# Longer DMA runs for q and k in a fused attention and gated-MLP kernel: four tokens to a run, order restored on chip

## Chip, cores and metric

The kernel runs on one core of a Trainium2 chip. The metric is the device time of one execution in microseconds (us); lower is better. Before the change it is 248.72 us, the median of three runs (248.6 to 251.48). A run counts as slow when it is over 1.5% above the fastest of the same kernel.

## The reference, cut to what matters

```python
def _attn_ref(q, k, v):                     # each (8, 8, 576, 64) float32: B, H, S, D
    # S is cut into chunks of 64 tokens; attention stays inside a chunk
    scores = scale * np.matmul(q_c, k_c.transpose(0, 1, 2, 4, 3))
    attn = softmax(scores)                   # (cut)
    return np.matmul(attn, v_c).reshape(B, H, S, D)

def reference(**kwargs):
    attn_out = _attn_ref(q, k, v)
    x = attn_out.transpose(0, 2, 1, 3).reshape(B, S, H * D)
    h = np.maximum(x @ w_in, 0.0); u, v = split(h)
    v_n = layer_norm(v)
    v_s = einsum('ts,bsd->btd', w_spatial, v_n) + b_spatial
    return (u * v_s) @ w_out                 # (8, 576, 512) float32
```

The inputs lie in HBM head by head: for one head, 64 floats (256 bytes) of a token are followed by those of the next token. The kernel works on tiles of 128 tokens with all 8 heads, 36 tiles in all. Four of them straddle two batches (576 is four and a half tiles) and are loaded in two pieces of 64 tokens.

## The kernel before

Loads, with tokens on the partitions, so that each contiguous run in HBM is 256 bytes:

```python
    att_in = pool("att_in", 4);  att_bf = pool("att_bf", 3);  osb_pool = pool("osb_pool", 4)
    # ...
    def load(t):
        for name, src in (("q", q), ("k", k), ("v", v)):
            f = att_in.tile([128, H, D], FP32, name=f"{name}f")
            for r0, n, b, s in pieces(t):
                nc.sync.dma_start(out=f[r0:r0 + n],
                                  in_=src[b, :, s:s + n, :].rearrange("h s d -> s h d"))
    # cast(t): GpSimd casts q, k, v to bf16
    # TR(t):   8 TensorE transposes of q and k into one PSUM tile; VectorE copies it out
    # QK(t):   16 score matmuls of 64x64; ScalarE takes the exponential
    # AV(t):   attention x v and the division; XT(t): 4 transposes, ScalarE copies to xT
    # HV, U:   first MLP matmuls;  LN, LN_apply: layer norm (apply is on GpSimd)
    # SP(b):   spatial matmuls of batch b;  FIN(t): last matmul, then
        o_sb = osb_pool.tile([128, d_model], FP32, name="o_sb")
        nc.scalar.copy(o_sb, po)
        nc.sync.dma_start(out=out_flat[t * 128:(t + 1) * 128, :], in_=o_sb)
```

The main loop fixes the order of TensorE and GpSimd by hand, with a model clock:

```python
        for s in range(NT + 3):
            if PRE <= s + PRE - 1 < NT and s > 0:
                load(s + PRE - 1)             # three tiles ahead
            while ln_todo:
                LN_apply(ln_todo.pop(0))      # GpSimd: waits for the statistics
            if 0 < s and s + 1 < NT:
                cast(s + 1)                   # GpSimd: one tile ahead
            # TR(s), XT, QK(s), AV(s-1), with HV / U / SP / FIN filled in between
```

The softmax here doesn't subtract the row's maximum and nothing guards it: scores larger than these inputs give would overflow.

## Time and profile before

| | before |
|---|---|
| median | 248.72 us |
| span of the profiled run | 247.3 us |
| TensorE busy | 204.3 us (83%) |
| DMA | 40.36 MB, mean 163 GB/s |
| GpSimd casts waiting for q and k | 18.7 us |

First the page's rows by time: 40 equal slices of the span, for each the busy share in tenths of TensorE (PE), of its granted clock (PEclk), of the 16 DMA engines on average, and the rate in GB/s; then the line of the hardware DMA queue (packets, megabytes, share of the time of 16 engines) and the issues (KB each, median us from issue to landing).

```profile
PE   0237756599199499999998899999979999999993
PEclk9999996559869979999999999999999999999999
DMA  8999999899249998069977799989738640050225
GB/s 155 211 189 208 175 219 209 181 219 211 50 101 213 188 220 179 34 185 214 193 184 176 166 204 245 255 180 191 196 107 190 111 170 3 0 209 5 85 85 212
...
q1 hardware_dynamic: 117696, 37.76, 69.7%
...
qf<-in_q_dram SPq DMA_DIRECT2D x32, 256.0 KB, 5.0
kf<-in_k_dram SPq DMA_DIRECT2D x32, 256.0 KB, 5.0
vf<-in_v_dram SPq DMA_DIRECT2D x32, 256.0 KB, 5.3
```

In the first quarter the DMA engines are full at some 200 GB/s while TensorE has gaps; from the middle on TensorE is nearly full. The table of stretches has the same in numbers (busy us with the count of instructions, of TensorE's matmuls and weight loads, VectorE, ScalarE and GpSimd in this order; then granted clock, DMA share, GB/s):

```profile
0.00:20.00 20.00, 5.54 (x77) 3.64 (x78) 2.58 (x11) 3.06 (x4) 7.92 (x18) 1.00 1.01 185
20.00:40.00 20.00, 13.00 (x164) 7.94 (x161) 8.76 (x19) 4.93 (x9) 10.21 (x17) 0.97 1.20 200
40.00:60.00 20.00, 16.39 (x177) 9.95 (x176) 7.61 (x17) 5.43 (x10) 4.30 (x7) 0.61 1.05 205
...
140.00:160.00 20.00, 19.91 (x257) 12.10 (x255) 11.94 (x31) 12.15 (x23) 8.02 (x14) 1.00 1.08 236
```

The table of waits (engine, line, tile, what it waited for: us in all, times, longest; POOL is GpSimd, ACT ScalarE, DVE VectorE, SPq the queue in which SyncE issues DMAs) shows how little the casts wait for q and k, how long GpSimd waits for layer-norm statistics, and that the copies into the output buffers wait for TensorE, not for stores:

```profile
POOL vn L258 <- DVE nmu L238: 64.3, 6, 16.2
...
POOL kb L141 <- DMA kf<-in_k_dram: 9.5, 8, 3.5
POOL qb L141 <- DMA qf<-in_q_dram: 9.2, 5, 4.5
...
ACT o_sb L300 <- PE big L297: 22.4, 34, 5.2
```

### The profile page before, as it was taken

How to read it: one execution, taken by the hardware profiler on the slowest of the kernel's cores; microseconds unless marked ns; L12 is line 12 of the kernel's file. 1: busy time of each engine (PE TensorE's matmuls, PEld its weight loads, DVE VectorE, ACT ScalarE, POOL GpSimd, SP SyncE). 2: the span in 40 equal slices, each digit the busy share in tenths (PEclk: the TensorE clock that was granted, in tenths of full speed). 3: DMA queues.
4: the chain of work that ended last, by engine and by line, in shares of the span. 5: the costliest groups of instructions: out<-in, count | busy, mean ns of one | idle time of the engine just before them, and what ended most of it. 6: DMA issues, size and time to landing. Idle time of an engine off the chain costs nothing.

```text
span 247.3 us, 5971 instructions
## 1 busy us (share of the span) xinstructions
PE 204.3 (83%) x2402; PEld 124.8 (50%) x2402; DVE 120.2 (49%) x305; ACT 105.6 (43%) x197; POOL 100.7 (41%) x166
## 2 busy tenths in 40 slices
PE   0237756599199499999998899999979999999993
PEld 0124435345155366566555555755556557446651
DVE  0124254434443667368635663874466548425530
ACT  2011230036227523762564276437643662864133
POOL 4515463300890794009801943395056400524000
PEclk9999996559869979999999999999999999999999
DMA  8999999899249998069977799989738640050225
GB/s 155 211 189 208 175 219 209 181 219 211 50 101 213 188 220 179 34 185 214 193 184 176 166 204 245 255 180 191 196 107 190 111 170 3 0 209 5 85 85 212
DMA packets 119994, 40.36 MB, mean 163 GB/s; under 512 B 113248, under 2 KB 115360, under 8 KB 119968
## 3 DMA queue, kind: packets, MB, share of 16 engines
q1 hardware_dynamic: 117696, 37.76, 69.7%
q0 software_dynamic: 2272, 2.24, 5.9%
q8 instruction: 18, 0.29, 0.5%
q14 instruction: 8, 0.07, 0.1%
HBM read 32.79 MB, written 9.44 MB: 171 GB/s over the span
## 4 chain that ended last, share of the span: by engine, by line
PE 49%; POOL 7%; issue 5%; DMA 4%; DVE 3%; SPq 2%; ACT 1%; POOLq 0%; ACTq 0%
PE big L281 13%; PE big L297 10%; PE big L265 9%; PE big L209 8%; DMA vf<-in_v_dram 4%; PE tr L151 4%; PE o L178 2%; PE tr L191 2%; PE sc L164 2%; SPq L132 2%; POOL vn L258 2%; POOL kb L141 2%; POOL qb L141 2%; DVE bst L215 1%; POOL vaug L141 1%
## 5 line engine op out<-in xcount | busy, mean ns | idle before, releaser
L258 POOL TENSOR_SCALAR vn<-v_relu,rstd,nmu 128x512 bf16<-128x512 f32 x32 | 25.1, 796 | 81.4 <-DVE nmu L238 64.3
L212 ACT ACTIVATE v_relu<-big 128x512 f32<-128x512 f32 x36 | 21.5, 597 | 58.9 <-PE big L209 49.7
L154 DVE COPY qkT<-tr 128x1024 bf16<-128x1024 bf16 x36 | 24.6, 684 | 44.2 <-PE tr L151 44.2
L281 PE MATMUL big<-wsf,vn 128*128 128x288 bf16 x256 | 40.5, 286 | 2.8 <-DVE gat L288 2.6
L215 DVE BATCH_NORM_STATS2 bst<-v_relu 128x6 f32<-128x512 f32 x36 | 24.9, 693 | 34.7 <-ACT v_relu L212 34.6
L209 PE MATMUL big<-w_in_sb,xT 128*128 128x512 bf16 x144 | 40.6, 414 | 0.0
L265 PE MATMUL big<-xT,w_in_sb 128*128 128x512 bf16 x144 | 35.6, 390 | 0.0
L297 PE MATMUL big<-w_out_sb,gat 128*128 128x512 bf16 (+1 forms) x160 | 34.5, 381 | 0.0
L288 DVE TENSOR_TENSOR gat<-big,uT 128x288 bf16<-128x288 f32 (+8 forms) x96 | 30.0, 351 | 8.2 <-PE big L281 7.2
L194 ACT COPY xT<-tr 128x512 bf16<-128x512 bf16 x36 | 21.0, 584 | 23.2 <-PE tr L191 23.1
L151 PE MATMUL tr<-identb,qb 128*128 128x128 bf16 x144 | 15.6, 238 | 18.3 <-POOL qb L141 17.2
L300 ACT COPY o_sb<-big 128x512 f32<-128x512 f32 x36 | 21.1, 586 | 22.4 <-PE big L297 22.4
L168 ACT ACTIVATE eT<-sc 128x512 bf16<-128x512 f32 x36 | 22.0, 611 | 17.5 <-PE sc L164 17.5
L281 PEld LDWEIGHTS <-vn 128*128 128x128 bf16 x256 | 23.7, 97 | 10.6 <-DVE gat L288 2.5
L141 POOL CAST qb<-qf 128x512 bf16<-128x512 f32 x36 | 22.0, 611 | 16.9 <-DMA qf<-in_q_dram 9.2
L141 POOL CAST vaug<-vf 128x512 bf16<-128x512 f32 x36 | 22.1, 615 | 13.8 <-DMA vf<-in_v_dram 13.8
L141 POOL CAST kb<-kf 128x512 bf16<-128x512 f32 x36 | 22.0, 612 | 13.5 <-DMA kf<-in_k_dram 9.5
L267 ACT ACTIVATE uT<-big 128x512 bf16<-128x512 f32 x36 | 21.3, 597 | 12.3 <-PE big L265 11.6
L184 DVE TENSOR_TENSOR x<-o,rz 128x512 bf16<-128x512 f32 x36 | 24.9, 691 | 0.9
L151 PEld LDWEIGHTS <-qb 128*128 128x128 bf16 x144 | 11.1, 105 | 25.2 <-POOL qb L141 19.2
L209 PEld LDWEIGHTS <-xT 128*128 128x128 bf16 x144 | 14.0, 104 | 14.3 <-issue 2.8
L265 PEld LDWEIGHTS <-w_in_sb 128*128 128x128 bf16 x144 | 13.5, 100 | 14.7 <-issue 1.6
(40 smaller groups left out, 195.0 us busy)
## 6 DMA issues: line engine op xcount, KB each, us to landing
out_dram<-o_sb SPq DMA_DIRECT2D x36, 256.0 KB, 2.1
qf<-in_q_dram SPq DMA_DIRECT2D x32, 256.0 KB, 5.0
kf<-in_k_dram SPq DMA_DIRECT2D x32, 256.0 KB, 5.0
vf<-in_v_dram SPq DMA_DIRECT2D x32, 256.0 KB, 5.3
qf<-in_q_dram SPq DMA_DIRECT2D x8, 128.0 KB, 4.6
kf<-in_k_dram SPq DMA_DIRECT2D x8, 128.0 KB, 4.1
vf<-in_v_dram SPq DMA_DIRECT2D x8, 128.0 KB, 4.2
ws_nat<-in_moe_w_spatial_dram POOLq DMA_DIRECT2D x1, 576.0 KB, 6.7
```

The lines of the kernel that those rows point to most:

```text
L141: nc.gpsimd.tensor_copy(dst, f32[name])
L151: nc.tensor.transpose(ps[:, c:c + 128], st[t][name][:, 2 * m:2 * m + 2, :].rearrange("p h d -> p (h d)"), identb)
L154: nc.vector.tensor_copy(qkT, ps)
L168: nc.scalar.activation(eT, sc[:, :, 0:256], AF.Exp, scale=att_scale)
L184: nc.vector.tensor_tensor(x, o[:, :, 0:64], rz.to_broadcast([128, H, D]), op=ALU.mult)
L209: nc.tensor.matmul(hv, xT[g][:, cb, r * 128:(r + 1) * 128], w_in_sb[:, cb, F:], start=(cb == 0), stop=(cb == 3))
L215: nc.vector.bn_stats(bst, vr)
L258: nc.gpsimd.tensor_scalar(y, vr, rstd[:, j:j + 1], nmu[:, j:j + 1], op0=ALU.mult, op1=ALU.add)
L265: nc.tensor.matmul(hu, w_in_sb[:, cb, fb * 128:(fb + 1) * 128], xT[g][:, cb, :], start=(cb == 0), stop=(cb == 3))
L281: nc.tensor.matmul(vs[:, 0:HS], lhsT, rhs, start=(i == 0), stop=(i == 4))
L288: nc.vector.tensor_tensor(gat[b][:, db, half * HS + done:half * HS + done + n], vs[:, done:done + n], uT[g][:, db, r:r + n], op=ALU.mult)
L297: nc.tensor.matmul(po[r0:r0 + n, :], gat[b][:, jb, s:s + n], w_out_sb[:, jb, :], start=(jb == 0), stop=(jb == 3))
```

## The change

The intent: q and k are loaded in runs of 1 KB, four consecutive tokens of one head, and a partition then holds four tokens of two heads. The order is put right again where k is copied out of PSUM, and by a permutation matrix (in place of the identity) in the transposes of the attention output. GpSimd casts two tiles ahead and before it normalises; the normalising is cut into single tiles; several pools are deeper; copies are shared out differently between VectorE and ScalarE; finished tiles have priority in the order.

The core of the diff (pools and the scheduling helpers cut):

```diff
-    att_bf = pool("att_bf", 3)
+    att_bf = pool("att_bf", 4)
-    relu_pool = pool("relu_pool", 8)
-    vn_pool = pool("vn_pool", 12)
+    relu_pool = pool("relu_pool", 12)
+    vn_pool = pool("vn_pool", 20)
+    permb = consts.tile([128, 128], BF16, name="permb")      # identity, columns permuted (cut)
     def load(t):
-        for name, src in (("q", q), ("k", k), ("v", v)):
-            f = att_in.tile([128, H, D], FP32, name=f"{name}f")
+        for name, src in (("q", q), ("k", k)):
+            f = att_in.tile([128, 2, 4 * D], FP32, name=f"{name}f")
             for r0, n, b, s in pieces(t):
-                nc.sync.dma_start(out=f[r0:r0 + n], in_=src[b, :, s:s + n, :].rearrange("h s d -> s h d"))
+                for e in (0, 1):
+                    nc.sync.dma_start(
+                        out=f[r0:r0 + n, e, :],
+                        in_=src[b, 4 * e:4 * e + 4, s:s + n, :].rearrange("h (p r) d -> h p (r d)", r=4))
+        # v is loaded as before
     def TR(t):
-        nc.vector.tensor_copy(qkT, ps)
+        nc.vector.tensor_copy(qT.rearrange("p r c -> p (r c)"), ps[:, 0:512])
+        kT = att_sb.tile([128, 128, 4], BF16, name="kT")
+        nc.scalar.copy(kT, ps[:, 512:1024].rearrange("p (r c) -> p c r", r=4))
     def QK(t):
-                                 qkT[p0:p0 + 64, 512 + col:512 + col + 64],
-                                 qkT[p0:p0 + 64, col:col + 64], start=True, stop=True)
+                                 kT[p0:p0 + 64, col:col + 16, :].rearrange("p l r -> p (l r)"),
+                                 qT[p0:p0 + 64, :, col:col + 16], start=True, stop=True)
     def XT(t):
-                                x[:, 2 * m:2 * m + 2, :].rearrange("p h d -> p (h d)"), identb)
+                                x[:, 2 * m:2 * m + 2, :].rearrange("p h d -> p (h d)"), permb)
     # main loop
-            while ln_todo:
-                LN_apply(ln_todo.pop(0))
-            if 0 < s and s + 1 < NT:
-                cast(s + 1)
+            if 0 < s and s + 2 < NT:
+                cast(s + 2)
+            for i in range(min(3, len(ln_todo))):
+                LN_apply(*ln_todo.pop(0))
```

More of the change, by code (lines that the diff above doesn't have):

```diff
@@ L47 @@
     persist = pool("persist", 1)
+    xT_pool = pool("xT_pool", 4)
+    uT_pool = pool("uT_pool", 6)
     att_in = pool("att_in", 4)
-    att_bf = pool("att_bf", 3)
+    att_bf = pool("att_bf", 4)
     att_sb = pool("att_sb", 3)
-    relu_pool = pool("relu_pool", 8)
-    vn_pool = pool("vn_pool", 12)
-    tail_pool = pool("tail_pool", 2)
+    relu_pool = pool("relu_pool", 12)
+    vn_pool = pool("vn_pool", 20)
+    tail_pool = pool("tail_pool", 3)
     stat_pool = pool("stat_pool", 3)
     bst_pool = pool("bst_pool", 4)
-    gat_pool = pool("gat_pool", 2)
+    gat_pool = pool("gat_pool", 3)
     osb_pool = pool("osb_pool", 4)
@@ L67 @@
     make_identity(nc, identb)
+    permb = consts.tile([128, 128], BF16, name="permb")
+    for c in (0, 1):
+        nc.vector.tensor_copy(permb[:, c * 64:c * 64 + 64].rearrange("p (l r) -> p l r", r=4),
+                              identb[:, c * 64:c * 64 + 64].rearrange("p (r l) -> p l r", r=4))
     eps_sb = consts.tile([128, 1], FP32, name="eps_sb")
@@ L74 @@
         nc.vector.memset(vaug[i][:, :, 64:65], 1.0)
-    xT = [persist.tile([128, 4, 512], BF16, name=f"xT{g}") for g in range(NG)]
-    uT = [persist.tile([128, 4, 512], BF16, name=f"uT{g}") for g in range(NG)]
+    xT, uT = {}, {}
     w_in_sb = persist.tile([128, 4, d_ff], BF16, name="w_in_sb")
@@ L109, in ws_transpose @@
             s0, n, dst = (512 if p == 0 else 0), 64, ws_tail[p]
-        ps = ps_tr.tile([128, 1024], BF16, name="tr")
+        ps = ps_big.tile([128, 1024], BF16, name="big")
         for tb in range(5):
@@ L114, in ws_transpose @@
                                 ws_nat[:m, tb, s0:s0 + n], identb[:m, :m])
-        nc.vector.tensor_copy(dst[:n, :], ps[:n, 0:S])
+        if (i + p) % 2:
+            nc.vector.tensor_copy(dst[:n, :], ps[:n, 0:S])
+        else:
+            nc.scalar.copy(dst[:n, :], ps[:n, 0:S])
     st = {}
@@ L128, in load @@
         f32 = {}
-        for name, src in (("q", q), ("k", k), ("v", v)):
-            f = att_in.tile([128, H, D], FP32, name=f"{name}f")
+        for name, src in (("q", q), ("k", k)):
+            f = att_in.tile([128, 2, 4 * D], FP32, name=f"{name}f")
             for r0, n, b, s in pieces(t):
-                nc.sync.dma_start(out=f[r0:r0 + n], in_=src[b, :, s:s + n, :].rearrange("h s d -> s h d"))
+                for e in (0, 1):
+                    nc.sync.dma_start(
+                        out=f[r0:r0 + n, e, :],
+                        in_=src[b, 4 * e:4 * e + 4, s:s + n, :].rearrange("h (p r) d -> h p (r d)", r=4))
             f32[name] = f
+        f = att_in.tile([128, H, D], FP32, name="vf")
+        for r0, n, b, s in pieces(t):
+            nc.sync.dma_start(out=f[r0:r0 + n], in_=v[b, :, s:s + n, :].rearrange("h s d -> s h d"))
+        f32["v"] = f
         st[t] = {"f32": f32}
@@ L137, in cast @@
         f32 = st[t].pop("f32")
-        qb = att_bf.tile([128, H, D], BF16, name="qb")
-        kb = att_bf.tile([128, H, D], BF16, name="kb")
+        qb = att_bf.tile([128, 4, 2, D], BF16, name="qb")
+        kb = att_bf.tile([128, 4, 2, D], BF16, name="kb")
         for dst, name in ((qb, "q"), (kb, "k"), (vaug[t % NVB][:, :, 0:64], "v")):
-            nc.gpsimd.tensor_copy(dst, f32[name])
+            x = f32[name]
+            nc.gpsimd.tensor_copy(dst, x if name == "v" else x.rearrange("p e (r d) -> p r e d", r=4))
             for f in after_each:
@@ L144, in cast, with cols @@
         st[t] = {"q": qb, "k": kb}
+    def cols(t, c, m):
+        return c * 64 + m * 16 if len(pieces(t)) == 2 else m * 32 + c * 16
     def TR(t):
@@ L148, in TR @@
         for i, name in enumerate(("q", "k")):
-            for m in range(4):
-                c = i * 512 + m * 128
+            for r in range(4):
+                c = i * 512 + r * 128
                 nc.tensor.transpose(ps[:, c:c + 128],
-                                    st[t][name][:, 2 * m:2 * m + 2, :].rearrange("p h d -> p (h d)"), identb)
-        qkT = att_sb.tile([128, 1024], BF16, name="qkT")
-        nc.vector.tensor_copy(qkT, ps)
-        st[t]["qkT"] = qkT
+                                    st[t][name][:, r].rearrange("p e d -> p (e d)"), identb)
+        qT = att_sb.tile([128, 4, 128], BF16, name="qT")
+        nc.vector.tensor_copy(qT.rearrange("p r c -> p (r c)"), ps[:, 0:512])
+        kT = att_sb.tile([128, 128, 4], BF16, name="kT")
+        nc.scalar.copy(kT, ps[:, 512:1024].rearrange("p (r c) -> p c r", r=4))
+        st[t]["qkT"] = (qT, kT)
     def QK(t):
-        qkT = st[t].pop("qkT")
+        qT, kT = st[t].pop("qkT")
         sc = ps_sc.tile([128, 2, 512], FP32, name="sc")
@@ L162, in QK @@
                 p0, c0 = e * 64, c * 64
-                col = m * 128 + c0
+                col = cols(t, c, m)
                 nc.tensor.matmul(sc[c0:c0 + 64, e, m * 64:m * 64 + 64],
-                                 qkT[p0:p0 + 64, 512 + col:512 + col + 64],
-                                 qkT[p0:p0 + 64, col:col + 64], start=True, stop=True)
+                                 kT[p0:p0 + 64, col:col + 16, :].rearrange("p l r -> p (l r)"),
+                                 qT[p0:p0 + 64, :, col:col + 16], start=True, stop=True)
         eT = att_sb.tile([128, 2, 256], BF16, name="eT")
@@ L178, in AV @@
                 nc.tensor.matmul(o[c0:c0 + 64, h, 0:65],
-                                 eT[c0:c0 + 64, h % 2, (h // 2) * 64:(h // 2) * 64 + 64],
+                                 eT[c0:c0 + 64, h // 4, (h % 4) * 64:(h % 4) * 64 + 64],
                                  va[c0:c0 + 64, h, :], start=True, stop=True)
@@ L191, in XT @@
             nc.tensor.transpose(ps[:, m * 128:(m + 1) * 128],
-                                x[:, 2 * m:2 * m + 2, :].rearrange("p h d -> p (h d)"), identb)
+                                x[:, 2 * m:2 * m + 2, :].rearrange("p h d -> p (h d)"), permb)
         g, r = divmod(t, 4)
-        nc.scalar.copy(xT[g][:, :, r * 128:(r + 1) * 128],
+        if r == 0:
+            xT[g] = xT_pool.tile([128, 4, 512], BF16, name="xT")
+        nc.vector.tensor_copy(xT[g][:, :, r * 128:(r + 1) * 128],
                        ps[:, 0:512].rearrange("p (m s) -> p m s", m=4))
@@ L240, in LN, with LN_apply @@
         ln_st[grp] = (k0, ts, rstd, nmu)
-    def LN_apply(grp):
-        k0, ts, rstd, nmu = ln_st.pop(grp)
-        for j, t in enumerate(ts):
-            vr = relu.pop(t)
-            if t - k0 == 4:
-                te = tail_pool.tile([128, F], BF16, name="tail_e")
-                to = tail_pool.tile([128, F], BF16, name="tail_o")
-                nc.gpsimd.memset(te[64:65, :], 1.0)
-                nc.gpsimd.memset(to[64:65, :], 1.0)
-                nc.gpsimd.tensor_scalar(te[0:64], vr[0:64], rstd[0:64, j:j + 1], nmu[0:64, j:j + 1],
-                                        op0=ALU.mult, op1=ALU.add)
-                nc.vector.tensor_scalar(to[0:64], vr[64:128], rstd[64:128, j:j + 1], nmu[64:128, j:j + 1],
-                                        op0=ALU.mult, op1=ALU.add)
-                tail[grp], tail[grp + 1] = te, to
-            else:
-                y = vn_pool.tile([128, F], BF16, name="vn")
-                nc.gpsimd.tensor_scalar(y, vr, rstd[:, j:j + 1], nmu[:, j:j + 1],
-                                        op0=ALU.mult, op1=ALU.add)
-                vn[t] = y
+    def LN_apply(grp, j):
+        k0, ts, rstd, nmu = ln_st[grp]
+        t = ts[j]
+        vr = relu.pop(t)
+        sc, bi = rstd[:, j:j + 1], nmu[:, j:j + 1]
+        if t - k0 == 4:
+            te = tail_pool.tile([128, F], BF16, name="tail_e")
+            to = tail_pool.tile([128, F], BF16, name="tail_o")
+            nc.gpsimd.memset(te[64:65, :], 1.0)
+            nc.gpsimd.memset(to[64:65, :], 1.0)
+            nc.gpsimd.tensor_scalar(te[0:64], vr[0:64], sc[0:64], bi[0:64], op0=ALU.mult, op1=ALU.add)
+            nc.vector.tensor_scalar(to[0:64], vr[64:128], sc[64:128], bi[64:128],
+                                    op0=ALU.mult, op1=ALU.add)
+            tail[grp], tail[grp + 1] = te, to
+        else:
+            y = vn_pool.tile([128, F], BF16, name="vn")
+            nc.gpsimd.tensor_scalar(y, vr, sc, bi, op0=ALU.mult, op1=ALU.add)
+            vn[t] = y
     def U(g, fb):
@@ L266, in U @@
                              start=(cb == 0), stop=(cb == 3))
+        if fb == 0:
+            uT[g] = uT_pool.tile([128, 4, 512], BF16, name="uT")
         nc.scalar.activation(uT[g][:, fb, :], hu, AF.Relu)
@@ L309, with push, can @@
     seq = [0]
-    def push(ready, cost, emit, after=None):
-        fifo.append([ready, seq[0], cost, emit, after])
+    def push(ready, cost, emit, after=None, pri=1, guard=None):
+        fifo.append([ready, (pri, seq[0]), cost, emit, after, guard])
         seq[0] += 1
+    def can(x):
+        return x[5] is None or x[5]()
     def run(item):
@@ L324, in fill @@
         while got < quota:
-            ok = [x for x in fifo if x[0] <= clock[0]]
+            ok = [x for x in fifo if x[0] <= clock[0] and can(x)]
             if not ok:
@@ L340, in after_hv @@
             LN(grp)
-            ln_todo.append(grp)
+            ln_todo.extend((grp, j) for j in range(n))
             ln_done.add(grp)
@@ L355, in try_sp @@
             sp_pushed.add(b)
-            ready = clock[0] + 6.0
+            ready = clock[0] + 12.0
             for half in (0, 1):
@@ L359, in try_sp, with gat_free @@
                     push(ready, 0.62, lambda b=b, half=half, db=db: SP(b, half, db),
-                         lambda b=b, half=half, db=db: after_sp(b, half, db))
-    fin_pushed = set()
+                         lambda b=b, half=half, db=db: after_sp(b, half, db),
+                         guard=lambda b=b: gat_free(b))
+    fin_pushed, fin_done = set(), set()
+    def gat_free(b):
+        c = b - 3
+        return c < 0 or all(t in fin_done for t in batch_tiles(c))
     def after_sp(b, half, db):
@@ L374, in after_sp @@
                 fin_pushed.add(t)
-                push(clock[0] + 1.2, 0.87, lambda t=t: FIN(t))
+                push(clock[0] + 1.2, 0.87, lambda t=t: FIN(t), lambda t=t: fin_done.add(t), pri=0)
     def after_u(g, fb):
@@ L389 @@
     PRE = 4
-    ARR = [6.7, 11.0, 18.0, 21.5, 25.0, 32.0, 35.5]
+    ARR = [6.0, 10.0, 15.0, 19.0, 23.0, 28.0, 32.0]
     def arrival(t):
-        return ARR[t] if t < len(ARR) else ARR[-1] + 3.5 * (t - len(ARR) + 1)
+        return ARR[t] if t < len(ARR) else ARR[-1] + 2.9 * (t - len(ARR) + 1)
     def after_cast0(name):
@@ L407 @@
         cast(1)
+        cast(2)
+        load_ws()
         for p in (0, 1):
             for i in range(5):
-                push(31.0, 0.4, lambda p=p, i=i: ws_transpose(p, i))
+                push(29.0, 0.4, lambda p=p, i=i: ws_transpose(p, i))
         xt_next = 0
@@ L414 @@
                 load(s + PRE - 1)
-            while ln_todo:
-                LN_apply(ln_todo.pop(0))
-            if 0 < s and s + 1 < NT:
-                cast(s + 1)
-                if s + 1 == 3:
-                    load_ws()
-                if s + 1 == 5:
+            if 0 < s and s + 2 < NT:
+                cast(s + 2)
+                if s + 2 == 4:
                     load_w_out()
+            for i in range(min(3, len(ln_todo))):
+                LN_apply(*ln_todo.pop(0))
             if s < NT:
@@ L450 @@
         while fifo:
-            ok = [x for x in fifo if x[0] <= clock[0]]
-            run(min(ok, key=lambda x: x[1]) if ok else min(fifo, key=lambda x: (x[0], x[1])))
+            can_run = [x for x in fifo if can(x)]
+            ok = [x for x in can_run if x[0] <= clock[0]]
+            run(min(ok, key=lambda x: x[1]) if ok else min(can_run, key=lambda x: (x[0], x[1])))
             while ln_todo:
-                LN_apply(ln_todo.pop(0))
+                LN_apply(*ln_todo.pop(0))
 _INS = ['q', 'k', 'v', 'moe_w_in', 'moe_w_spatial', 'moe_b_spatial', 'moe_w_out']
```

## The prediction

> **What bounds the kernel now.** Two stages. In the table of stretches, the DMA share is 1.01, 1.20 and 1.05 in the first three 20 us, at only 185 to 205 GB/s: 110,592 of the 119,994 packets are the 256-byte runs of q, k and v, 18 ns each at the median (mean 21) in the list of packets. A 768 KB tile takes 3.9 us, TensorE is busy 35 of 60 us, and its clock falls to 0.61. From 100 us on TensorE is busy 18 to 20 of every 20 us: it is the bound. The chain of waits agrees: TensorE 49%, DMA 4%. The last v tile is cast at 196 us; the TensorE order then holds 44 us of work, until 243 us.
>
> **What the change means to do.** 512 KB of each tile go in 1 KB runs: 18,432 packets replace 73,728. A line through the measured 18 ns (256 B) and 83 ns (2 KB stores) gives an estimate of 46 ns for 1 KB; on 16 engines that is 1.5 us for q and k, 2.8 us a tile with v. Were that all, I would expect about 225 us. Copies swap between VectorE and ScalarE, neither the bound; TensorE keeps its 2,402 matmuls.
>
> **Why I expect the opposite.** The new source pattern is (4 heads, 32 rows, 1 KB), its target 128 partitions. The Trainium skill, "DMA: Bandwidth & Descriptors", section "Why a DMA increments its semaphore by 16 and not by 1", says the DMA is spread over the largest k up to 16 that divides the slowest dimension of both sides, on the lowest-numbered k engines. Before, 128 and 128 give 16; the trace agrees: 117,696 hardware-queue packets are 115,200 of data and 2,496 = 16 x 156 completions. Now 4 and 128 give k = 4. No run shows it yet. So q and k go through engines 0 to 3 alone.
>
> Costs on those engines, a tile: 128 packets of 1 KB at 45 ns = 5.8 us; 64 v packets at 19 ns = 1.2 us; together 7.0 us (3.9 before). 36 tiles: 253 us. About 22 output tiles stored meanwhile (8 packets of 84 ns) add up to 15 us, the weights (132 packets of 98 ns) about 8 us. The last load lands near 276 us. It is all on the critical path: TensorE's 5.2 us of work a tile is shorter. After the last tile the TensorE order still holds 44 us (counted from it, same as before), plus cast, store and drain about 5 us.
>
> **Prediction: 324 us; 8 in 10 between 298 and 348. Faster by over 2%: 0.06; within 2%: 0.01; slower: 0.93.**
>
> **What would show it.** The hardware queue holds 61,760 packets (160 q and k issues with 4 completions each), not 63,680 (16 each). Mean rate falls to about 125 GB/s, the queue's share of 16 engines to about 38% although the loads bound the kernel.  The q and k casts on GpSimd wait for DMA, over 100 us in all (18.7 before); TensorE falls to near 65% busy.  Last q cast near 275 us (194 before).
>
> **What would make it wrong.** If the queue spreads by partitions after all (k = 16), TensorE bounds all but the start and the time is 215 to 235 us. If 1 KB packets take 40 or 52 ns, the time moves by -23 or +32 us. If stores and weights overlap with loads, 15 us less. If GpSimd, normalising only behind casts two tiles ahead, delays TensorE, some us more.

## The result, and the profile after

The changed kernel is correct and takes 350.19 us (median of four runs, 348.62 to 354.06), against 248.66 us of the kernel before on the same chip. The ratio is 1.4025 (95% interval 1.3891 to 1.4159). Ratios here are the mean time of one kernel's fast runs over that of the other's in the same rounds, so not quite the ratio of the quoted medians. The direction and the slower loads were predicted; the time is 2 us above the predicted range, because one step of the sum, what follows the last load, was wrong (see below).

The profiled run of the changed kernel (354.06 us) fell 1.6% above the fastest. Differences of that size are not read from it.

```profile
PE   0114356592593678777765039999730059999995
PEclk9999998787577559989897558999985559999999
DMA  3945456333343433434534445444334442101324
GB/s 77 170 107 129 99 125 135 105 107 103 105 122 100 112 106 108 127 108 150 157 106 115 119 154 181 132 127 150 101 107 124 118 154 84 37 3 61 121 88 151
...
q1 hardware_dynamic: 61760, 37.76, 36.7%
...
DMA 51%; PE 21%; SPq 18%; POOL 5%; issue 2%; ACT 0%; POOLq 0%; ACTq 0%
```

The last line is the chain of waits by engine. The hardware queue holds 61,760 packets, exactly the number that 4 completions for each of the 160 q and k loads make; 16 would make 63,680. The mean share of the DMA engines has fallen to mostly 3 to 5 tenths, and yet DMA is half of the chain that ended last. A mean over 16 engines that shows 0.4 can be four engines that are full and twelve that have little to do. The trace does not name the engine of a packet, but its list of packets tells how many 1 KB packets were under way at once: four for half of the time in which there were any, and more than five for 3% of it. (In the two-engine run below it is two for 77% of that time and never more than four; in the sixteen-engine run it is up to 24.)

The stretches and the waits that answer to those shown of before:

```profile
40.00:60.00 20.00, 10.87 (x111) 6.01 (x112) 5.33 (x13) 4.75 (x9) 4.79 (x8) 0.91 0.53 114
...
140.00:160.00 20.00, 15.43 (x178) 8.92 (x180) 9.80 (x26) 9.51 (x18) 4.92 (x8) 0.91 0.42 114
...
260.00:280.00 20.00, 0.00 (x0) 0.00 (x0) 0.00 (x0) 0.00 (x0) 4.98 (x9) 0.53 0.41 111
```

```profile
POOL kb L160 <- DMA kf<-in_k_dram: 84.2, 33, 6.7
...
POOL qb L160 <- DMA qf<-in_q_dram: 71.6, 30, 6.0
...
ACT o_sb L329 <- DMA out_dram<-o_sb: 52.0, 3, 28.5
...
PE big L310 <- ACT o_sb L329: 46.0, 2, 27.4
```

The casts now wait 155.8 us for q and k (18.7 before): that was predicted. What was not: from 260 to 280 us no compute engine but GpSimd does anything, although tiles keep arriving. The last two lines say why. TensorE waits for a PSUM buffer that ScalarE has not emptied, and ScalarE waits for one of the four output buffers, whose store has not landed. The timeline at that place shows what held the store (start, us, engine, line, operation; in brackets the idle time before and its releaser). The first line is the copy that fills the last of the four buffers:

```profile
254.63 0.58 ACT L329 COPY o_sb<-big 128x512 f32<-128x512 f32 x1 [0.28 <-PE big L326]
...
263.61 4.47 SPq L143 DMA_DIRECT2D qf<-in_q_dram  x2
...
270.58 4.87 SPq L143 DMA_DIRECT2D qf<-in_q_dram  x2
...
277.19 0.77 SPq L149 DMA_DIRECT2D vf<-in_v_dram  x1
...
278.05 8.45 SPq L330 DMA_DIRECT2D out_dram<-o_sb  x5
...
285.56 0.58 ACT L329 COPY o_sb<-big 128x512 f32<-128x512 f32 x1 [28.46 <-DMA out_dram<-o_sb]
...
286.19 1.12 PE L310 MATMUL big<-wsf,vn 128*128 128x288 bf16 x4 [27.41 <-ACT o_sb L329]
```

SyncE issues in its order, and in this order the loads of the last tiles come before these stores: the four buffers were filled between 247.1 and 255.2 us, and the first of their stores was issued at 278.05 us. The pair of q loads takes 4.5 to 4.9 us to issue from 256 to 275 us (about 1.2 us in the corrected kernel of the first experiment), which I read as the queue of the full engines pushing back; no run tests that reading. (The waits of TensorE for output copies are 46.0 us in two stalls: this one and an earlier one of 18.6 us.)

When does a tile arrive? The starts of the v casts, in us, taken from the trace's timeline (first, every fifth after it, last), with the end of the span:

```
                    tile 0     5    10    15    20    25    30    35 | span
before                 6.8  35.2  70.5  89.6 119.1 143.5 168.2 195.9 | 247.3
changed               11.5  59.6  96.5 132.9 168.3 207.3 248.4 284.9 | 352.3
```

From tile 6 to tile 20 the changed kernel gets a tile every 7.0 to 7.9 us, close to the 7.0 us of the prediction.

And the packets of the hardware queue, from the list of packets in the trace (ns):

```
                 size    count   10th pct  median  mean
before           256 B  110592      18       18    21.0
changed          256 B   36864      18       18    18.5
changed         1024 B   18432      46       52    53.1
before, stores  2048 B    4608      82       84    89.4
```

### The profile page after: what moved, and what is told of

Its sections match the earlier page's. It is cut to its first block, busy times and chain, and to the rows that moved or that the text cites. A ratio compares the mean times of both kernels' runs of the same rounds, so it can differ in the third digit from the quotient of the medians.

```text
span 352.3 us, 6109 instructions
## 1 busy us (share of the span) xinstructions
PE 217.2 (62%) x2368; PEld 131.7 (37%) x2402; DVE 124.1 (35%) x338; ACT 110.2 (31%) x202; POOL 103.2 (29%) x166
## 3 DMA queue, kind: packets, MB, share of 16 engines
q1 hardware_dynamic: 61760, 37.76, 36.7%
## 4 chain that ended last, share of the span: by engine, by line
DMA 51%; PE 21%; SPq 18%; POOL 5%; issue 2%; ACT 0%; POOLq 0%; ACTq 0%
DMA vf<-in_v_dram 24%; SPq L143 18%; DMA kf<-in_k_dram 17%; DMA qf<-in_q_dram 8%; PE big L310 6%; PE big L326 5%; PE big L292 4%; PE big L237 2%; DMA out_dram<-o_sb 2%; POOL vaug L160 2%; POOL kb L160 1%; POOL vn L286 1%; PE tr L174 1%; SPq L149 1%; PE big L119 1%
## 5 line engine op out<-in xcount | busy, mean ns | idle before, releaser
L310 PE MATMUL big<-wsf,vn 128*128 128x288 bf16 x256 | 45.9, 311 | 46.0 <-ACT o_sb L329 46.0
L317 DVE TENSOR_TENSOR gat<-big,uT 128x288 bf16<-128x288 f32 (+8 forms) x96 | 30.8, 353 | 73.0 <-PE big L310 71.5
L177 DVE COPY qT<-tr 128x512 bf16<-128x512 bf16 x36 | 15.2, 421 | 93.7 <-PE tr L174 93.7
L174 PE MATMUL tr<-identb,kb 128*128 128x128 bf16 x144 | 17.2, 255 | 48.8 <-POOL kb L160 48.8
L310 PEld LDWEIGHTS <-vn 128*128 128x128 bf16 x256 | 26.0, 105 | 56.1 <-issue 46.2
L179 ACT COPY kT<-tr 128x512 bf16<-128x512 bf16 x36 | 21.0, 584 | 83.1 <-DVE qT L177 83.1
L329 ACT COPY o_sb<-big 128x512 f32<-128x512 f32 x36 | 21.0, 584 | 73.8 <-DMA out_dram<-o_sb 52.0
L174 PEld LDWEIGHTS <-kb 128*128 128x128 bf16 x144 | 10.5, 111 | 53.5 <-POOL kb L160 53.5
L174 PE MATMUL tr<-identb,qb 128*128 128x128 bf16 x144 | 16.4, 246 | 17.9 <-POOL qb L160 16.9
L217 PE MATMUL tr<-permb,x 128*128 128x128 bf16 x144 | 16.6, 249 | 9.3 <-ACT kT L179 4.7
```

Source lines behind the costliest of these rows:

```text
L174: nc.tensor.transpose(ps[:, c:c + 128], st[t][name][:, r].rearrange("p e d -> p (e d)"), identb)
L310: nc.tensor.matmul(vs[:, 0:HS], lhsT, rhs, start=(i == 0), stop=(i == 4))
L317: nc.vector.tensor_tensor(gat[b][:, db, half * HS + done:half * HS + done + n], vs[:, done:done + n], uT[g][:, db, r:r + n], op=ALU.mult)
```

## The experiments

Theory A: q and k go through four of the sixteen DMA engines, because the slowest dimension of the new source pattern is 4. Rival B: the loads are slow because there are more issues of a costlier form on SyncE, or because of 1 KB runs as such. Rival C: the new order of instructions costs the time.

### Rows first (k16)

```diff
-     in_=src[b, 4 * e:4 * e + 4, s:s + n, :].rearrange("h (p r) d -> h p (r d)", r=4))
+     in_=src[b, 4 * e:4 * e + 4, s:s + n, :].rearrange("h (p r) d -> p h (r d)", r=4))
-        return c * 64 + m * 16 if len(pieces(t)) == 2 else m * 32 + c * 16
+        return slice(c * 64 + m, c * 64 + m + 61, 4)
-        kT = att_sb.tile([128, 128, 4], BF16, name="kT")
-        nc.scalar.copy(kT, ps[:, 512:1024].rearrange("p (r c) -> p c r", r=4))
+        kT = att_sb.tile([128, 4, 32, 4], BF16, name="kT")
+        nc.scalar.copy(kT, ps[:, 512:1024].rearrange("p (r l m) -> p m l r", r=4, m=4))
```

(The score matmuls take the matching slices.)

> The only edit: the source of the q and k loads is walked rows first, heads second (32 rows, 4 heads, 1 KB instead of 4 heads, 32 rows, 1 KB), and the k copy and the q columns of the score matmuls follow the new order. Same number of issues, same bytes, same 1 KB runs, same order of instructions on every engine. Theory A (the old pattern put q and k on 4 of the 16 DMA engines): 63,680 packets in the hardware queue, a tile loads in about 3 us, TensorE bounds all but the start; 225 us, between 215 and 238. Theory B (it is the SyncE issues, five unhurried ones a tile at 1.4 us each, or the 1 KB pattern itself, that slow the loads): stays between 330 and 355.

Measured: correct, 229.57 us (228.81 to 235.18), ratio to before 0.921 (0.9117 to 0.9304). The queue's line:

```profile
q1 hardware_dynamic: 63680, 37.76, 59.0%
```

Same bytes, same runs, same number of issues, same instruction order, 121 us less than the changed kernel (350.19 - 229.57, across rounds; both ratios are to the same kernel before). Theory A holds and B falls for these 121 us. That the result also beats the kernel before is looked at further down.

### Two engines (k2)

```diff
                 for e in (0, 1):
-                    nc.sync.dma_start(out=f[r0:r0 + n, e, :], in_=src[b, 4 * e:4 * e + 4, ...)
+                    for u in (0, 1):
+                        nc.sync.dma_start(out=f[r0 + u * n // 2:r0 + (u + 1) * n // 2, e, :],
+                                          in_=src[b, 4 * e + 2 * u:4 * e + 2 * u + 2, ...)
```

> The changed kernel with each q and k load cut in two, two heads each, so that the slowest dimension of the source is 2. Theory A: engines 0 and 1 carry 256 packets of 1 KB a tile at 52 ns, 13.3 us, and 64 v packets, 1.2 us: 14.5 us a tile, 522 us for the loads, and 50 to 70 us after them; 585 us, between 545 and 625; 62,400 - 320 x 2 completions counted: 61,760 packets again (320 issues with 2 each). Theory B (issues bound): four issues more a tile at about 0.7 to 1.4 us, 450 to 530 us.

Measured: 541.72 us (two runs), and 61,760 packets as expected:

```profile
q1 hardware_dynamic: 61760, 37.76, 23.1%
```

Four and two engines make the same count here (160 x 4 = 320 x 2 completions), so it is the time that tells them apart. The time is 3 us under the range of A; tiles arrive mostly every 12.9 to 14.1 us, not 14.5, because the expectation took the mean packet of 52 ns where packets overlap a little. 229.6, 350.2 and 541.7 us for 16, 4 and 2 engines is the order that A asks for.

### The kernel before, with other divisors (before_124 and its control before_112)

```diff
-                nc.sync.dma_start(out=f[r0:r0 + n], in_=src[b, :, s:s + n, :].rearrange("h s d -> s h d"))
+                cuts = [(0, 124), (124, 4)] if n == 128 and name != "v" else [(0, n)]
+                for a, w in cuts:
+                    nc.sync.dma_start(out=f[r0 + a:r0 + a + w],
+                                      in_=src[b, :, s + a:s + a + w, :].rearrange("h s d -> s h d"))
```

The control has `[(0, 112), (112, 16)]` in the same place.

> The kernel before, with each full q and k load of 128 rows cut into one of 124 rows and one of 4; runs of 256 bytes as before. Theory A (engines used = the largest divisor up to 16 of the slowest dimension, here 4): engines 0 to 3 carry 512 packets of 18 ns for q and k and 64 for v, 10.4 us a full tile; 32 such tiles, 4 tiles as before, 29 us of weights, stores and start: the last load lands near 378 us; 430 us in all, between 405 and 460. Hardware-queue packets: 105,472 less because nothing but the completions change: 115,200 of data, 64 x 2 x 4 + 24 x 16 + 32 x 16 + 36 x 16 = 1,984 completions. Rival B (more issues or 1 KB runs are what costs): 248 to 262 us, as its twin with 112 and 16 rows.

(The number 105,472 in that text is a slip; the sum behind it gives 117,184.)

> The control: the kernel before with each full q and k load cut into one of 112 rows and one of 16, so as many issues as with 124 and 4, but 16 divides both. Theory A: 16 engines everywhere, 245 to 258 us. Rival B (number of issues): as its twin.

Measured: 407.02 us for 124 and 4 (two runs, ratio 1.6368), 254.05 us for 112 and 16 (two runs, ratio 1.0216). The queue's lines, of the first and then of the control:

```profile
q1 hardware_dynamic: 117184, 37.76, 43.2%
```

```profile
q1 hardware_dynamic: 118720, 37.76, 72.2%
```

With 256-byte runs and nothing else of the change, the old kernel becomes 64% slower when 124 rows are moved in one load and 4 in another, and 2% slower with 112 and 16. The number of issues is the same. So it is the divisor that does it. The control's 6 us over the kernel before are clear of noise (ratio 1.0125 to 1.0307); I put them down to the extra issues, which no run isolates.

### The rest of the change, with the old loads (sched_only)

```diff
-            f = att_in.tile([128, 2, 4 * D], FP32, name=f"{name}f")      # 1 KB runs (cut)
+            f = att_in.tile([128, H, D], FP32, name=f"{name}f")
+                nc.sync.dma_start(out=f[r0:r0 + n], in_=src[b, :, s:s + n, :].rearrange("h s d -> s h d"))
-        nc.scalar.copy(kT, ps[:, 512:1024].rearrange("p (r c) -> p c r", r=4))
+        nc.scalar.copy(kT, ps[:, 512:1024])
-                                ..., permb)
+                                ..., identb)
```

> The changed kernel with q, k loaded as before (256-byte runs, 16 engines, no permutation), so only the rest of the change is left: pools, order, casts two tiles ahead, swapped copies. Theory A: the loads are as before, so the time is near before, 240 to 256 us. Rival C (the new order of instructions, not the loads, costs most of the 100 us): above 300 us.

Measured: 228.82 us (227.52 to 230.32), ratio 0.9182 (0.9109 to 0.9256): faster than either theory said. Rival C is refuted, in fact reversed: the new order and pools gain 20 us by themselves. And since the corrected kernel with 1 KB runs takes 229.57 us, the 1 KB runs gain nothing on top of it. They do load sooner: the last v cast starts at 161.3 us in the corrected kernel and at 173.1 us here, yet both spans end at 227 us. In both, TensorE is most of the chain that ended last (first the corrected kernel, then this one):

```profile
PE 74%; DMA 8%; SPq 5%; ACT 4%; DVE 3%; POOL 2%; issue 2%; ACTq 0%; POOLq 0%
```

```profile
PE 70%; DVE 11%; DMA 8%; SPq 5%; ACT 4%; issue 1%; POOL 1%; ACTq 0%; POOLq 0%
```

### Casts ahead alone, in the kernel before (before_cast2)

```diff
-            while ln_todo:
-                LN_apply(ln_todo.pop(0))
-            if 0 < s and s + 1 < NT:
-                cast(s + 1)
+            if 0 < s and s + 2 < NT:
+                cast(s + 2)
+            while ln_todo:
+                LN_apply(ln_todo.pop(0))
```

(with one more buffer for the cast tiles, and the weight loads that hang on the casts moved along)

> The kernel before with one part of the change: the casts run two tiles ahead and stand before the normalising on GpSimd (one more buffer for the cast tiles); loads, copies, pools and TensorE order as before. Theory S (of the 20 us that the rest of the change gains, most comes from GpSimd no longer holding loads back behind normalising that waits for statistics): 230 to 238 us. Rival (the deeper pools and the new TensorE order gain it): 244 to 252 us.

Measured: 239.2 us (238.41 to 241.72), ratio 0.9636 (0.956 to 0.9713). It is a miss for the theory, just above its range and below the rival's: 9 of the 20 us, less than half. TensorE's order is unchanged here (the traces show the same order of all 2,402 weight loads), so this part comes from the new order on GpSimd, with the extra buffer and the earlier weight loads that came along. The last v cast starts at 187.1 us instead of 195.9, and GpSimd's wait for the statistics is down:

```profile
POOL vn L258 <- DVE nmu L238: 26.3, 3, 17.4
```

(64.3 us before). The size of that wait alone decides little: the corrected kernel has 40.6 us of it and takes 229.57 us. What differs in the code is whether casts stand behind it. Which of the deeper pools, the finer normalising, the new TensorE order and the swapped copies gives the other 11 us was not tried and stays open.

### Where did the missed time come from? Stores on another queue (k4_act_store)

This and the next run change the changed kernel, to find why it took longer than predicted.

```diff
-        nc.sync.dma_start(out=out_flat[t * 128:(t + 1) * 128, :], in_=o_sb)
+        nc.scalar.dma_start(out=out_flat[t * 128:(t + 1) * 128, :], in_=o_sb)
```

> The changed kernel with the output stores issued from ScalarE's queue instead of SyncE's. Theory T (the 27 us in which TensorE stood still near 260 us came from stores stuck in the SyncE order behind loads of later tiles, and added to the end): the stall goes, the last load still lands near 284 us, then 44 us of TensorE order and about 5 us: 325 to 338 us. Rival (TensorE would have waited for the last tiles anyway, so the stall costs nothing): 345 to 352 us.

Measured: 348.59 us (347.43 to 349.16), ratio 1.398, so no gain. The stall has only moved. In the waits of this run:

```profile
ACT o_sb L329 <- DMA kf<-in_k_dram: 44.9, 4, 17.4
...
ACT o_sb L329 <- DMA qf<-in_q_dram: 15.8, 2, 8.1
```

ScalarE's copy into an output buffer now waits, by the profile, for loads. The trace has the reason: all DMAs that SyncE and ScalarE issue in this program share eight completion counters (semaphores 101 to 108), and ScalarE's order has a wait for one of them before 21 of the 36 stores. The output copy that ends at 266.0 us, for example, has its store issued only at 273.7 us, right after a wait for counter 106, which loads use as well, and the next copy stands behind that store. The theory that the SyncE order alone holds the stores fell; that stores are held behind loads, by one means or the other, did not.

### More output buffers (k4_osb11)

```diff
-    osb_pool = pool("osb_pool", 4)
+    osb_pool = pool("osb_pool", 11)
```

> The changed kernel with 11 output buffers in place of 4; the order of every engine is the same. Theory T2 (TensorE fell behind the loads because output tiles wait for their stores, and stores are held by loads queued before them or by the completion counters they share): TensorE keeps up with the loads, the last load lands near 285 us as before, 44 us of TensorE order and 5 us follow: 328 to 340 us. Rival (something else holds TensorE back, as the run with the stores on ScalarE's queue suggested): 345 to 351 us.

Measured: 329.59 us (327.43 to 331.3), ratio 1.3225 (1.3119 to 1.3331): 20.6 us less than the changed kernel. The waits for stores are gone: of the waits of the output copies the table of waits has only that for TensorE itself, and the stretch in which everything stood still is busy:

```profile
ACT o_sb L329 <- PE big L326: 22.5, 24, 4.4
```

```profile
260.00:280.00 20.00, 13.93 (x171) 8.39 (x176) 7.01 (x18) 8.74 (x17) 5.53 (x9) 0.93 0.43 117
```

The last v cast starts at 283.1 us (284.9 in the changed kernel), so the loads are as slow as ever, and the span ends 46.4 us later (329.5 - 283.1). In the changed kernel it ended 67.4 us later (352.3 - 284.9).

### The loads alone (loads_k4, loads_k16, loads_256, loads_k16_2q)

Four kernels with a wrong result: only the loads, and one tile stored. The core of the edit:

```diff
-        for t in range(PRE):
-            load(t)
-        # casts, matmuls, normalising, stores (all cut)
+        for t in range(NT):
+            load(t)
+    nc.sync.dma_start(out=out_flat[0:128, :], in_=st[NT - 1]["f32"]["v"].rearrange("p h d -> p (h d)"))
```

> Wrong result on purpose: the changed kernel's loads of q, k and v alone, four buffers each, nothing computed, one tile stored. Theory A: 128 packets of 46 ns and 64 of 18 ns a tile on engines 0 to 3, 7.0 us a tile as in the full kernel between tiles 6 and 20: 254 us and 5 us for start and end: 255 to 266 us. So weights and stores put 25 to 30 us before the last load of the full kernel.

Measured: 264.83 us (one run); in the list of packets the tiles follow each other at a median of 7.05 us. In the full kernel the last v packet lands some 25 us later (284.2 against 259.4 us from the start of the span). The gaps in the full kernel say where: its first five are 12.5, 7.1, 11.5, 7.3 and 10.4 us, 13 us more than five of 7.1, while the weights are loaded; the eleven from tile 20 to 31, in which stores go between, add 10 us.

> Wrong result on purpose: the same loads with the rows walked first (16 engines). Theory A: 32 packets of 46 ns and 64 of 18 ns an engine and tile are 2.6 us, the five issues of about 0.55 us are 2.8 us: 95 to 115 us.

> Wrong result on purpose: the loads of the kernel before alone (256-byte runs, 16 engines). 192 packets of 18 to 21 ns an engine and tile, 3.5 to 4.0 us: 130 to 148 us. With the run before this says what 1 KB runs are worth when all engines carry them, and why the full kernel, where TensorE needs 5.2 us a tile, does not gain from it.

Measured: 137.75 us and 140.4 us (one run each). The second came as expected, the first missed by far: with all 16 engines, 1 KB runs load hardly faster than 256-byte runs. The timeline of SyncE in loads_k16 shows why:

```profile
22.69 0.59 SPq L149 DMA_DIRECT2D vf<-in_v_dram  x1
23.32 1.24 SPq L143 DMA_DIRECT2D qf<-in_q_dram  x2
24.61 1.25 SPq L143 DMA_DIRECT2D kf<-in_k_dram  x2
25.90 0.59 SPq L149 DMA_DIRECT2D vf<-in_v_dram  x1
26.53 1.24 SPq L143 DMA_DIRECT2D qf<-in_q_dram  x2
```

The issues stand back to back, about 0.6 us each, with no wait before them: a tile takes five of them, 3.2 us, and a straddling tile ten. From the first of the 200 issues to the last are 128 of the 136 us, 0.64 us each with the gap. So the gain of the longer runs seems to have turned into issue time; the next run tests that.

> Wrong result on purpose: the loads alone on 16 engines in 1 KB runs, those of k issued by ScalarE's queue instead of SyncE's. If the 138 us of the run with one queue are its 200 issues of 0.6 us back to back on SyncE (0.63 x 200 = 126), SyncE now has 120 issues and the engines 2.6 us a tile: 96 to 110 us. If they are the DMA engines' own limit for this pattern, it stays at 132 to 138.

```diff
-                    nc.sync.dma_start(
+                    (nc.sync if name == "q" else nc.scalar).dma_start(
```

Measured: 124.26 us (one run). It is 14 us less, so issue time was part of the bound; but it misses the 96 to 110 us. Now the DMA engines are full, at a mean of 0.9 to 1.0 in the stretches between 10 and 110 us, and the q packets of 1 KB take 57 ns on average (median 46, one in a hundred 295 ns). 32 of them and 64 v packets of 18.2 ns an engine and tile are 3.0 us, 108 us for 36 tiles. Why some packets are so much longer with all engines at work, the runs do not show.

## Why the prediction was right or wrong

**The bound before: right for the start, incomplete for the middle.** The packets and the full TensorE are as read. But the loads of the kernel before were held not only by 256-byte packets: they alone take 140.4 us, and in the full kernel the last tile was cast at 195.9 us. GpSimd, which freed the load buffers, stood 64.3 us behind the layer-norm statistics. The prediction listed that wait nowhere.

**Four engines: right, and shown.** 61,760 packets as predicted; four 1 KB packets at once for half of the time that any are under way; 7.05 us a tile against 7.0; rows first takes it away; 124 and 4 rows bring it into the old kernel. The mean rate was 115 GB/s (predicted 125), the queue's share 36.7% (38%), TensorE 62% busy (65%), the casts' waits 155.8 us (over 100).

**The last load: 285 us instead of 276.** The term for the loads held (36 x 7.05 = 254 us). The stores before it cost 10 us (up to 15 predicted). The weights cost about 13 us, not 8 (the prediction's own figures, 132 packets of 98 ns, already make 12.9 us). And the prediction had no term for the start: the first tile's v is cast at 11.5 us, 4 us more than one tile's 7.1. What is left, some 3 us, is in slightly longer gaps of the other tiles.

**The step that failed: "After the last tile the TensorE order still holds 44 us (counted from it, same as before), plus cast, store and drain about 5 us."** From the last v cast to the end it took 67.4 us in the profiled run, not 49. The length of the order was right, but it assumed that TensorE had done all that stands before the last tile by then. It had not: with four output buffers, and stores held behind slow loads, it stood still for 27 us while tiles arrived (259 to 286 us, "PE big L310 <- ACT o_sb L329"), and had to catch up afterwards. With 11 buffers, the same order and the same loads, the rest is 46.4 us and the time 329.59 us, inside the predicted range. This term accounts for about 20 us of the 26 us between 324 and 350, the last load for the others.

**The packet's size: right as a rate.** The guess of 45 ns for 1 KB is the 46 ns of the fastest packets. The mean was 53 ns, but packets overlap a little (in the loads alone, 128 of 52.3 ns and 64 of 18.0 ns would make 7.8 us a tile, and a tile came every 7.05 us), so the gap between tiles gives the rate.

**"If k = 16, 215 to 235 us": the number was right (229.57), the reason was not.** The prediction gave the gain to the loads, so hitting it was in part luck. The run with the old loads and the rest of the change takes 228.82 us, the same within noise. TensorE's work, 5.4 us a tile (195.8 us busy for 36 tiles in the corrected kernel), hides loads of 3.9 us a tile as well as faster ones once they can run ahead; that is how I read the two runs. The two best versions are the rest of the change with the old loads, and the corrected loads; nothing shows a difference between them, and the first is simpler.

## What to carry to other kernels

Before making DMA runs longer, look at the slowest dimension of both sides of each load as the instruction has it: the number of DMA engines follows from it, and putting heads before rows left q and k a quarter of the engines here, while the mean DMA share looked relaxed. When one resource becomes slower, ask which small ring (here four output buffers) now couples two streams, and do not count on the other stream to have kept up. And run the rest of a change without its headline part: here all of the gain was in the rest.

## What the Trainium skill lacked or had wrong

- "DMA: Bandwidth & Descriptors", section "Why a DMA increments its semaphore by 16 and not by 1": its rule for the number of engines was borne out, with packet counts that fit 2, 4 and 16 engines exactly (61,760, 61,760 and 63,680 packets; 117,184 with 124 and 4 rows). That they are the lowest-numbered engines, no run here shows. It does not say what breaking the rule costs: 541.72, 350.19 and 229.57 us for 2, 4 and 16 engines.
- The same page, section "Issuing engines are not separate DMA queues", calls the time to start a DMA usually small relative to the DMA itself. Here an issue of a 128 KB load took 0.59 us on SyncE, more than the 8 x 46 ns = 0.37 us of its packets on an engine (an estimate from the measured packet), though less than its 3.2 us from issue to landing; 200 issues back to back made up 128 of 136 us, and moving 80 of them to ScalarE's queue took the time from 137.75 to 124.26 us.
- The same page, section "Specifications", gives a minimum transfer for line rate of 512 B and about 27 GiB/s an engine. In runs of 1 KB, a packet took 46 ns at best, 22 GB/s, and 57 ns on average with all engines at work (the loads on two queues), so runs of twice that minimum did not reach the engine's rate here.
- "Perfetto Trace Analysis", section "Identifying the Most-Contended Engine", does warn that occupancy misleads with 16 DMA engines, and sends the reader to HBM utilization first. It has no example of a few engines that are full, and here the bandwidth looks as relaxed as the share: 114 GB/s at 0.42 between 140 and 160 us, while the loads bound the kernel.
